# GpSimd clamps the weights' high words, and one fixed order of all operations: forgetting attention with two feed-forward layers

## The chip, the cores and the metric

The kernel runs on one core of a Trainium2 chip. The metric is the device time of one execution in microseconds (us). One further execution is recorded by the hardware profiler; its span runs from the first to the last instruction on the core, and all rows below come from it.

## The reference

```python
def _attn_ref(q, k, v, s):                      # batch 4, 8 heads, 576 positions, 64 wide
    scores = scale * np.matmul(q, k.transpose(0, 1, 3, 2))
    cum = np.cumsum(np.maximum(s, 0.0), axis=-1)
    bias = -(cum[:, :, :, None] - cum[:, :, None, :])
    scores = np.where(causal, -1000000000.0, scores + np.minimum(bias, 0.0))
    ...
    return np.matmul(softmax(scores), v)

def _moe_ref(x, w_in, w_out):                   # 2304 tokens, 512 -> 2048 -> 512
    h = x @ w_in
    g = np.where(h >= 1, h, np.where(h <= -1, 0.0, (h + 1) ** 2 / 4))
    return g @ w_out

def _moe2_ref(x, w_a, w_b, w_out):              # 512 -> 1536 -> 512
    return ((x @ w_a) * (x @ w_b)) @ w_out
```

The weights come as 64-bit floating point. The program has to turn each into a 32-bit value on the chip, and it multiplies in a reduced 32-bit format: a value is split into a high and a low part, and a product takes three passes (high by high, high by low, low by high).

## The kernel before, in words

The work is three stages that overlap: attention for four batches of 576 positions (ATT), layer one for batches 0 and 1, then 2 and 3, and layer two in the same pairs (PHASES). Attention goes by heads: a head's q and k are loaded in 64 rows each, scores come out of TensorE in row blocks of 116 (lines 982 and 991, the first head's at 961 and 971), VectorE adds the mask and takes the row's least value (line 1014), ScalarE takes the exponential (line 1029), TensorE turns the result (line 1055), ScalarE or VectorE copies it out, and TensorE multiplies it with v (line 1098). From batch 2 on the finished rows are parked in memory and fetched again. In the first heads q and k go to TensorE as they are; later ones are split into high and low parts, by a conversion on ScalarE or GpSimd (line 675 is GpSimd's) and a subtraction on VectorE (line 938).

The layers are tiled by blocks of 128 hidden columns and by batch. A plain product is in line 1351. For some phases a product of 2 by 2 blocks is done with seven products in place of eight (line 1508): it needs sums of the input blocks, "forms" (made at lines 1466 to 1479), and sums of the weight blocks, "sets" (lines 1429 to 1434), and its seven results are put together by ScalarE and VectorE (lines 1525 to 1540). y is summed in SBUF (line 1612).

**The weights.** values_of (from line 1261) makes 32-bit values of one weight tile of 128 by 512. SP loads the 64-bit words into one of two places of a tile `conv`. ScalarE scales the low words (line 1292) and takes the absolute value of the high words (line 1294). VectorE clamps that between two limits (line 1296, `wclamp`), shifts it (1298), puts the sign in (1300), and adds the low word's part (1302). load_unit then splits the value into high and low (a cast on ScalarE or GpSimd, and a subtraction on VectorE at line 1330) and stores it, so that later phases load it without a conversion (`whl`). keep_raw stores the value itself. There are 68 such tiles, from 13.8 to 681.0 us. For layer one GpSimd also makes sums (lines 1245 and 1252). The tile for the values has two places, and the one for the low words has one.

**The order of the work.** Nothing is issued as it is written: `op` records each operation with the engines that it may run on and their costs, what it reads and writes, and a key from the table KEYS. There are 4,604 operations, and 112 of them may run on either of two engines (mostly ScalarE or GpSimd for casts, and ScalarE or VectorE for copies). `Plan.run` keeps a clock for each engine, worked out from the costs. At each step it looks, for each engine, through up to 30 (LOOK) operations that are ready, in order of their keys, asks for places in their tiles (Room.find, Banks.find), and issues the one that can start first. The keys are thus preferences, and the plan's clocks decide; an operation for two engines goes to the one that can take it first. Each engine then runs its own instructions in the order of issue. SP starts all loads and stores, 618 of them, and waits at the head of its queue for the place or the value that a transfer needs.

Where the plan sees TensorE standing for more than 2 us (FILL_FROM), it puts in matmuls of zeros (`fill`, line 763). At the start there are 12 of the same kind (line 809). The plan adds up to 0.5 us to a VectorE operation marked `port` that begins while GpSimd is at work.

Of the kernel before, what the change touches and what calls it, by code (L numbers as in the profile page):

```python
# [44 lines left out]
LOOK = 30  # L45
# [4 lines left out]
    -46.11, -45.72, -39.66, -46.69, -57.55, -59.4, -56.04, -53.81, -44.56, -25.01, 13.24, 16.59, 24.15, 38.58, 45.28, 37.13, 42.56, 33.78, -57.18,  # L50
    -50.52, -31.43, -35.21, -34.65, -32.74, -24.3, -25.04, -29.4, -50.41, 4.82, 8.8, 14.61, 19.55, 6.46, 8.15, 20.64, 10.74, 3.69, 7.7, 15.87, 22.6,
    6.82, 9.05, 19.81, 21.57, 3.47, 9.85, 13.94, 21.33, -44.91, -5.67, -39.52, -3.58, -34.78, -3.2, -42.69, -6.95, -49, -0.1, -35.09, -3.13, -4.51,
    -4.13, 6.33, -5.33, 13.97, 21.29, 12.47, 12.1, 20.26, 15.12, 10.52, 15.27, 15.16, 19.71, 19.27, 15.23, 16.72, 20.55, 22.35, -15.22, 2.3, -14.99,
    3.83, 0.58, 12.31, 3.97, 8.12, 6.13, 3.35, 9.65, -1.29, 10.75, 10.41, -1.96, 6.13, 32.03, 16.69, 14.21, 39.19, 42.64, 33.41, 44.85, 22.96, 16.18,
    3.78, 33.95, 9.53, 17.76, 18.01, 18.93, 17.39, 15.29, 21.48, 18, 18.32, 24.48, 23.68, 18.74, 26.16, 31.41, 23.41, 31.3, 21.59, 15.71, 20.23, 20.2,
    21.89, 27.66, 27.38, 28.16, 26.5, 27.83, 30.34, 32.19, 7.5, 8.54, 12.39, 17.34, 24.92, 30.83, 30.7, 26.56, 33.78, 62.22, 24.92, 29.96, 30.15,
    29.06, 35.74, 38.18, 31.05, 33.72, 40.23, 28.23, 35.36, 25.88, 31.71, 31.12, 28.75, 32.54, 34.37, 32.14, 33.45, 33.79, 32.87, 34.73, 35.8, 28.08,
    39.72, 51.79, 36.92, 42.88, 40.47, 40.03, 63.22, 63.61, 50.35, 55.27, 45.07, 66.12, 4.68, 30.82, 34.42, 31.83, 33.79, 37.18, 37.81, 33.92, 42.45,
    34.2, 34.73, 41.93, 29.32, 32.17, 35.55, 35.88, 37.84, 53.62, 41.86, 34.58, 45.47, 52.47, 47.3, 49.65, 47.66, 53.67, 47.59, 56.45, 34.97, 31.09,
    31.02, 63.46, 40.36, 43.13, 43.1, 41.69, 40.02, 35.97, 41.77, 36.29, 44.98, 53.74, 38.2, 40.1, 39.37, 38.98, 49.82, 35.41, 28.27, 39.35, 30.19,  # L60
    48.82, 51.73, 45.29, 86.7, 48.99, 87.18, 50.86, 98.48, 52.54, 90.5, 57.23, 59.37, 36.65, 59.32, 66.24, 64.7, 66.85, 75.86, 69.08, 38.41, 39.3,
    42.42, 58.92, 19.71, 51.32, 57.22, 55.6, 41.45, 45.4, 67.54, 49.1, 49.91, 51.38, 50.01, 51.21, 55.65, 47.88, 49.6, 47.56, 54.2, 53.52, 57.64,
    50.6, 58.48, 58.4, 57.77, 59.16, 59.25, 62.82, 59.31, 45.63, 45.32, 37.43, 41.76, 57.93, 50.56, 56, 55.9, 48.96, 49.79, 56.09, 50.71, 59.97, 56.1,
    52.7, 65.04, 56.78, 55.07, 59.19, 58.36, 59.73, 60.56, 61.13, 61.1, 63.13, 64.23, 57.95, 59.15, 62.09, 63.15, 61.91, 56.32, 62.52, 61.54, 64.55,
    72.33, 40.14, 39.97, 66.28, 83.48, 72.91, 70.44, 51.46, 64.33, 62.3, 43.01, 66.78, 55.99, 54.16, 52.65, 59.4, 57.74, 53.82, 55.88, 61.76, 62.22,
    64.21, 62.58, 71.71, 67.62, 66.91, 58.78, 62.27, 61.43, 60.49, 63.07, 62.38, 68.54, 64.37, 71.1, 73.37, 69.15, 69.69, 70.85, 69.44, 48.71, 48.24,
    50.63, 64.2, 63.95, 64.56, 60.47, 67.79, 63.68, 66.66, 67.58, 74.58, 63.81, 73.31, 78.28, 68.8, 70.72, 70.88, 75.42, 61.14, 83.49, 68.94, 99.75,
    77.62, 87.21, 69.19, 86.41, 73.37, 86.79, 75.64, 91.76, 71.77, 83.29, 88.14, 84.7, 76.73, 93.72, 97.96, 100.6, 123.75, 124.45, 116.61, 114.63,
    105.58, 72.95, 73.48, 74.13, 74.29, 11.62, 17.68, 76.99, 86.6, 80.99, 76.28, 41.42, 84.47, 85.97, 84.62, 88.57, 90.99, 83.27, 98.68, 100.82,
    99.04, 99.89, 104.26, 101.37, 87.54, 79.89, 87.96, 79.4, 85.79, 94.98, 88.86, 102.14, 112.47, 103.93, 101.45, 92.09, 91.25, 92.23, 91.45, 74.84,  # L70
    64.62, 66.5, 67.37, 15.19, 22.88, 69.62, 75.56, 74.22, 96.12, 91.55, 96.81, 103.14, 76.8, 75.99, 83.43, 96.23, 99.89, 100.63, 99.4, 108.88,
    103.21, 97.26, 101.77, 104.73, 93.59, 71.05, 77.84, 67.27, 90.89, 97.58, 97.72, 93.55, 99.29, 102.74, 101.71, 97.81, 101.09, 105.61, 110.28,
    113.17, 111.59, 111.21, 123.39, 114.14, 123.27, 120.72, 118.67, 131.24, 134.85, 77.19, 73.91, 76.07, 78.5, 119.81, 99.61, 82.68, 94.07, 102.28,
    119.27, 69.6, 99.96, 100.92, 98.79, 99.63, 98.71, 114.33, 104.04, 102.52, 104.03, 104.57, 101.75, 100.84, 108.42, 106.57, 105.58, 103.1, 100.91,
    105.38, 101.71, 110.41, 106.85, 113.64, 108.8, 112.16, 108.86, 112.06, 106.96, 83.67, 85.51, 83.63, 85.47, 92.75, 94.29, 101.18, 102.36, 98.83,
    107.29, 107.32, 131.07, 111.75, 107.66, 105.68, 107.78, 116.1, 106.05, 118.75, 119.12, 119.04, 117.49, 115.45, 114.67, 129.55, 110.61, 107.04,
    113.05, 103.56, 114.89, 110.15, 106.36, 116.4, 105.22, 112.23, 107.83, 114.58, 106.64, 110.57, 104.2, 93.45, 115.23, 120.86, 125.08, 130.76,
    137.55, 135.92, 144.81, 165.18, 149.75, 102.16, 103.03, 113.69, 102.17, 102.9, 113.95, 112.51, 107.47, 102.27, 138.94, 101.43, 116.55, 126.98,
    120.59, 120.8, 130.48, 123.95, 123.07, 127.17, 136.29, 126.6, 135.51, 132.23, 128.5, 135.58, 131.72, 115.08, 106.74, 114.86, 113.18, 117.38,
    116.36, 113, 120.38, 122.04, 123.21, 123.17, 121.42, 108.12, 108.72, 109.94, 111.53, 119.99, 119.65, 127.95, 111.49, 135.2, 131.84, 130.3, 135.93,  # L80
    130.68, 126.36, 126.68, 134.88, 130.44, 128.59, 134.52, 132.29, 131.49, 147.24, 134.01, 138.83, 130.58, 148.14, 150.72, 134.08, 141.8, 151.68,
    144.98, 137.76, 144.37, 143.27, 149.78, 141.08, 149.12, 146.53, 150.86, 151.55, 153.79, 120.68, 133.07, 134.55, 134.03, 162.07, 161.05, 157.58,
    157.26, 159.28, 143.71, 131.34, 145.57, 145.64, 127.95, 127.44, 117.72, 144.13, 149.16, 161.69, 127.37, 149.51, 157.82, 165.83, 135.77, 138.2,
    166.31, 141.07, 140.22, 165.27, 147.53, 155.07, 175.32, 147.73, 148.66, 178.99, 151.57, 161.32, 156.92, 153.86, 152.62, 153.3, 158.61, 156.96,
    158.51, 162.77, 158.95, 169.03, 98.59, 81.85, 100.79, 103.95, 144.02, 142.7, 134.54, 154.81, 138.84, 147.06, 156.07, 146.8, 160.61, 158.7, 151.64,
    158.13, 157.88, 145.1, 165.1, 159.1, 149.29, 153.92, 163.9, 155, 160.61, 163.79, 168.82, 165.69, 158.39, 167.74, 184.37, 156.42, 167.52, 160.03,
# [1679 lines left out]
```

## Time and profile before

| | |
|---|---|
| median of 3 runs | 1028.62 us (1025.46 to 1031.27) |
| profiled execution, its time | 1028.6 us |
| profiled execution, its span | 1026.9 us |
| mean granted clock of TensorE | 0.998 |
| TensorE busy | 1012.2 us |
| VectorE busy | 815.9 us |
| ScalarE busy | 613.1 us |
| GpSimd busy | 95.2 us |

A row of the trace names a line of the kernel, an engine (PE is TensorE's multiplication, PEld its weight load, DVE VectorE, ACT ScalarE, POOL GpSimd, SP the queue of loads and stores), the tile written and the tile read, and the shape. "before" an arrow stands idle time and what ended it. Idle time costs only where the engine is the one that sets the end.

### The profile page before, as it was taken

The page shows a single profiled execution, that of the slowest core. Times are in us where ns is not written, and L with a number is a line of the kernel's source. Part 1 is how long each engine was busy: PE and PEld are TensorE (multiplying, and loading weights), DVE is VectorE, ACT ScalarE, POOL GpSimd, SP SyncE. Part 2 cuts the span into 40 slices and gives each one's busy share as a digit, 9 for nine tenths or more (in the row PEclk, how much of TensorE's full clock was granted, in tenths as well). Part 3 has the DMA queues.
Part 4 walks back from the last instruction along what each step waited for, and adds up shares of the span by engine and source line. Part 5 has one row for each costly group of instructions (what it writes and reads, how often), then busy time and mean ns, then how long its engine had stood idle before and what let it go on. Part 6 is the DMA issues. An engine that isn't in the chain of part 4 may idle for free.

```text
span 1026.9 us, 20033 instructions
## 1 busy us (share of the span) xinstructions
PE 1012.2 (99%) x7548; PEld 960.1 (94%) x7548; DVE 815.9 (79%) x1629; ACT 613.1 (60%) x1307; POOL 95.2 (9%) x130
## 2 busy tenths in 40 slices
PE   8999999999999999999999999999999999999998
PEld 5768889899999988999999999999999999999998
DVE  7888888767788979878888998897788985766563
ACT  5888888787686974786666535554333444452230
POOL 3232342010202202000000000000000000000000
PEclk9999999999999999999999999999999999999999
DMA  5676678876676668668373553443133331030012
GB/s 147 207 239 190 197 239 279 250 235 201 184 244 229 212 203 282 230 199 272 138 237 104 170 177 116 133 165 112 42 126 109 113 106 41 22 124 22 21 63 93
DMA packets 83321, 166.25 MB, mean 162 GB/s; under 512 B 9260, under 2 KB 40236, under 8 KB 83224
## 3 DMA queue, kind: packets, MB, share of 16 engines
q1 hardware_dynamic: 83128, 164.82, 49.0%
q8 instruction: 59, 0.97, 0.4%
q14 instruction: 38, 0.31, 0.1%
q10 hardware_dynamic: 96, 0.15, 0.0%
HBM read 119.57 MB, written 44.82 MB: 160 GB/s over the span
## 4 chain that ended last, share of the span: by engine, by line
PE 89%; DVE 3%; DMA 3%; ACT 2%; POOL 1%; issue 1%; SPq 1%; POOLq 0%; DVEq 0%
PE pp L1351 29%; PE pp L1508 20%; PE ps L1508 15%; PE ps L1351 11%; PE ps L1098 4%; PE ps L1055 4%; PE ps L991 2%; PE ps L982 2%; PE pp L991 1%; PE pp L982 1%; DMA conv<-in_w_in 1%; DMA qkraw<-in_qk 1%; DMA v<-in_v 1%; POOL g L1466 1%; SPq L683 1%
## 5 line engine op out<-in xcount | busy, mean ns | idle before, releaser
L1351 PE MATMUL pp<-g,whl 128*128 128x288 f32 x1788 | 261.1, 297 | 2.4 <-DVE y L1612 1.7
L1351 PEld LDWEIGHTS pp<-g,whl 128*128 128x128 f32 x1788 | 243.6, 188 | 3.6 <-issue 2.1
L1508 PE MATMUL pp<-form,set 128*128 128x288 f32 x1536 | 235.0, 297 | 0.1
L1508 PEld LDWEIGHTS pp<-form,set 128*128 128x128 f32 x1536 | 213.6, 188 | 1.3 <-DVE ct L1540 0.4
L1508 PE MATMUL ps<-form,set 128*128 128x288 f32 x1152 | 175.2, 296 | 0.8 <-DVE ct L1527 0.5
L1508 PEld LDWEIGHTS ps<-form,set 128*128 128x128 f32 x1152 | 160.3, 188 | 1.3 <-DVE ct L1527 0.8
L1351 PE MATMUL ps<-g,whl 128*128 128x288 f32 x900 | 137.5, 296 | 0.0
L1351 PEld LDWEIGHTS ps<-g,whl 128*128 128x128 f32 x900 | 125.4, 188 | 0.3
L1351 PE MATMUL pp<-x,whl 128*128 128x288 f32 x720 | 105.7, 300 | 0.3 <-DVE mx L1014 0.3
L1351 PEld LDWEIGHTS pp<-x,whl 128*128 128x128 f32 x720 | 98.3, 190 | 1.9 <-issue 0.6
L1029 ACT ACTIVATE p<-p,mx 116x232 f32<-116x232 f32 (+4 forms) x140 | 81.5, 583 | 8.9 <-DVE mx L1014 8.2
L1527 DVE TENSOR_TENSOR ct<-ps,ct 128x288 f32<-128x288 f32 x128 | 57.7, 455 | 35.8 <-ACT ct L1536 17.3
L1536 ACT COPY ct<-ps 128x576 f32<-128x576 f32 x64 | 41.1, 641 | 66.6 <-PE ps L1508 52.2
L1433 ACT CAST set<-sums 128x1024 fp32r<-128x1024 f32 (+1 forms) x56 | 53.6, 957 | 44.7 <-DVE sums L1429 22.2
L1549 ACT CAST g<-ct 128x576 fp32r<-128x576 f32 x80 | 51.2, 674 | 44.5 <-PE pp L1351 19.1
L671 ACT COPY pt<-ps 116x448 f32<-116x448 f32 (+5 forms) x175 | 64.5, 399 | 14.5 <-PE ps L1055 13.0
L1434 DVE TENSOR_TENSOR set<-sums,set 128x1024 fp32r<-128x1024 f32 (+1 forms) x56 | 61.9, 1106 | 8.9 <-ACT set L1433 8.1
L1612 DVE TENSOR_TENSOR y<-pp,y 128x576 f32<-128x576 f32 x70 | 52.7, 754 | 18.6 <-PE pp L1351 18.3
L1550 DVE TENSOR_TENSOR g<-ct,g 128x576 fp32r<-128x576 f32 x80 | 58.1, 754 | 8.4 <-ACT g L1549 7.7
L1540 DVE TENSOR_TENSOR ct<-pp,ct 128x576 f32<-128x576 f32 x64 | 48.2, 754 | 17.0 <-PE pp L1508 16.6
L1014 DVE CUSTOM_DVE_ANT_0 p<-ps,hide 116x348 f32<-116x348 f32 (+3 forms) x112 | 49.5, 453 | 15.1 <-PE ps L991 11.2
L1055 PE MATMUL ps<-ident,p 116*116 116x116 f32 (+2 forms) x420 | 60.1, 264 | 1.2 <-ACT xraw L1108 0.5
(123 smaller groups left out, 1390.7 us busy)
## 6 DMA issues: line engine op xcount, KB each, us to landing
whl<-keep_out SPq DMA_DIRECT2D x48, 512.0 KB
qkraw<-in_qk SPq DMA_DIRECT2D x108, 144.0 KB
conv<-in_w_out SPq DMA_DIRECT2D x28, 512.0 KB
keep_out<-whl SPq DMA_DIRECT2D x28, 512.0 KB
conv<-in_w_in SPq DMA_DIRECT2D x16, 512.0 KB
keep_in<-whl SPq DMA_DIRECT2D x16, 512.0 KB
g<-park SPq DMA_DIRECT2D x22, 288.0 KB
conv<-in_w_a SPq DMA_DIRECT2D x24, 256.0 KB
```

Of the source, the lines that this page charges most:

```text
L671: nc.scalar.copy(o, i)
L1014: nc.vector.tensor_tensor_reduce(out=psl(pref.t)[:r].rearrange("q (g n) -> q g n", g=parts), in0=pv()[:r, :parts, :w], in1=hide[:r, lag : ...
L1029: nc.scalar.activation(p, p, AF.Exp, bias=mx.t[:r], scale=-1.0, accum_out=sm.t[:r, h % 2, i : i + 1])
L1055: nc.tensor.transpose(pt.t[: rows[j], (j - j0) * QT : (j - j0) * QT + r], psl(pref.t)[:r, QT * j : QT * j + rows[j]], ident[:r, :r],)
L1351: nc.tensor.matmul(bank_of(ps, a)[:, :HN], w(wu), x(xu)[:, a * HN : (a + 1) * HN], start=(k == 0 and t == 0), stop=(k == len(terms) - 1 an ...
L1433: op({ACT: act(256 * n)}, k, lambda e: nc.scalar.copy(part(0, j0, n), src()), reads, slots, name="sethi")
L1434: op({DVE: tt(256 * n)}, k, lambda e: nc.vector.tensor_tensor(part(1, j0, n), src(), f32(part(0, j0, n)), op=ALU.subtract), reads, slots, ...
L1508: nc.tensor.matmul(at(to), by_pair(st.t)[:, w, wu, g], forms[b, layer, g].t[:, x, xu], start=fresh and k == 0, stop=k == len(terms) - 1, s ...
L1527: op({DVE: tt(HN)}, k, lambda e: nc.vector.tensor_tensor(cut(f, f), at(to), cut(f, f), op=ALU.add), [to, *shared], [(c, q)], name="partadd")
L1549: op({ACT: act(S)}, k, lambda e, f=f: nc.scalar.copy(g[f].t[:, 0], t.t[:, f]), need[f], [(g[f], 0)], name="ghi")
L1550: op({DVE: tt(S)}, k, lambda e, f=f: nc.vector.tensor_tensor(g[f].t[:, 1], t.t[:, f], f32(g[f].t[:, 0]), op=ALU.subtract), [*need[f], (g[f ...
L1612: nc.vector.tensor_tensor(o, i, o, op=ALU.add)
```

## The change

Two things change. The clamp of the high words (line 1296) is issued on GpSimd and not on VectorE, with the same two limits and the same shape, and it is no longer marked `port`. And the plan no longer searches: KEYS holds a whole number for each operation, every number once, TURNS says for each of the 112 operations with two engines which it takes, and `Plan.run` issues all operations in the order of their numbers. It still keeps the clocks, which now serve to choose places in tiles and banks and to find gaps for the matmuls of zeros; an operation that would come ahead of one that it needs, or for which there is no place, stops the build.

The numbers are new, not those of the former plan's outcome. Set side by side, TensorE's 1,318 operations are 5 places from their former place on average and 35 at most. GpSimd's operations go from 121 to 188, VectorE's from 1,412 to 1,344, ScalarE's from 1,135 to 1,136; of the two-engine operations 49 change sides, 22 of them copies between ScalarE and VectorE.

```diff
-LOOK = 30
...
 KEYS = (
...
+TURNS = (
+    "0100011001011011000101000100100101000001001010011001111101111011011111011111110011011001101110011011000111111101"
 )
...
         key = KEYS[len(self.ops)]
         o.engs, o.key, o.fn, o.move, o.name, o.port, o.lat = engs, key, fn, move, name, port, lat
+        o.by = 0
+        if len(engs) > 1:
+            o.by = int(TURNS[self.turn])
+            self.turn += 1
...
-        while True:
-            best = None
-            for e, todo in ready.items():
...
-            (t, key, o, places), e = best
+        for count, o in enumerate(sorted(self.ops, key=lambda o: o.key)):
+            assert o.waits == 0, f"{o.name} ({count}) comes too early"
+            e = list(o.engs)[o.by]
+            t = max(clock[e], o.ready)
+            places = []
+            ahead = {}
+            for r in o.refs:
+                if r.t is None:
+                    r.room.now = clock[e]
+                    at = r.room.find(r, ahead.get(id(r.room), 0))
+                    assert at is not None, f"{o.name} ({count}) has no place"
+                    ahead[id(r.room)] = ahead.get(id(r.room), 0) + 1
+                    places.append((r, at[1]))
+                    t = max(t, at[0])
             for r, at in places:
                 r.room.take(r, at)
...
-        op({DVE: ts(512)}, k, lambda e: vec.tensor_scalar(wr.t, wr.t, HIGH_MOST, HIGH_LEAST, op0=ALU.min, op1=ALU.max),
-            (), [(wr, 0)], name="wclamp", port=True)
+        op({POOL: pool(512)}, k, lambda e: nc.gpsimd.tensor_scalar(wr.t, wr.t, HIGH_MOST, HIGH_LEAST, op0=ALU.min, op1=ALU.max),
+            (), [(wr, 0)], name="wclamp")
```

## Rows read from the trace of the kernel before

**Rows 1.** The page's table of engines: busy time, share of the span, instructions.

```profile
PE 1012.2 (99%) x7548; PEld 960.1 (94%) x7548; DVE 815.9 (79%) x1629; ACT 613.1 (60%) x1307; POOL 95.2 (9%) x130
```

**Rows 2.** Busy time of each engine by stretch; columns as its first line says.

```profile
core 0: us, PE busy (x) PEld busy (x) DVE busy (x) ACT busy (x) POOL busy (x), PEclk, DMA share, GB/s
0.00:425.00 425.00, 413.64 (x3054) 362.69 (x3055) 353.36 (x797) 328.47 (x801) 95.23 (x130) 1.00 0.69 223
425.00:1000.00 575.00, 575.00 (x4320) 574.17 (x4319) 453.62 (x819) 283.34 (x506) 0.00 (x0) 1.00 0.36 120
76.00:79.40 3.40, 3.15 (x15) 2.65 (x16) 3.05 (x11) 1.69 (x6) 0.04 (x1) 0.50 0.81 236
389.00:407.00 18.00, 16.30 (x114) 14.23 (x112) 17.93 (x36) 7.75 (x16) 2.22 (x2) 1.00 0.75 252
```

**Rows 3.** TensorE's waits: for whom, us in total, times, longest.

```profile
PE ps L1098 <- DMA v<-in_v: 1.7, 1, 1.7
PE pp L1351 <- DVE y L1612: 1.7, 1, 1.7
PE ps L809 <- DVE zeros L804: 1.3, 1, 1.3
...
PE ps L991 <- DVE early L1387: 0.9, 1, 0.9
PE pp L1351 <- DVE mx L1014: 0.9, 2, 0.7
PE ps L961 <- DMA qkraw<-in_qk: 0.8, 1, 0.8
PE ps L1508 <- DVE ct L1527: 0.5, 1, 0.5
...
PE ps L1351 <- DVE mx L1014: 0.2, 1, 0.2
```

**Rows 4.** TensorE's timeline: start, us, instructions merged, idle time before them.

```profile
1.26 4.27 PE L809 MATMUL ps<-zeros 128*128 128x512 bf16 x12 [1.26 <-DVE zeros L804]
...
76.25 1.43 PE L1098 MATMUL ps<-pt,v 116*64 116x232 f32 x8 [1.74 <-DMA v<-in_v]
...
389.79 3.63 PE L763 MATMUL ps<-zeros 128*128 128x512 bf16 x16
...
401.47 3.42 PE L1351 MATMUL pp<-g,whl 128*128 128x288 f32 x24 [1.70 <-DVE y L1612]
...
1020.18 3.34 PE L1351 MATMUL ps<-g,whl 128*128 128x288 f32 x24
```

**Rows 5.** The clamp, line 1296: ns least/median/most, first and last start.

```profile
L1296 DVE TENSOR_SCALAR conv<-conv x68: 366/421/954, 13.8 to 681.0; 128x512 f32<-128x512 f32 x68
```

**Rows 6.** Busy time of line 1296 alone by stretch.

```profile
0.00:425.00 425.00, 20.13 (x44) 1.00 0.69 223
425.00:700.00 275.00, 10.12 (x24) 1.00 0.53 174
375.00:425.00 50.00, 1.65 (x4) 1.00 0.74 257
```

**Rows 7.** GpSimd's copies and conversions of 128x512: ns least/median/most.

```profile
L1245 POOL COPY g<-conv x8: 610/612/616, 41.1 to 338.4; 128x512 f32<-128x512 f32 x8
...
L675 POOL CAST whl<-conv x10: 609/614/1877, 22.2 to 167.0; 128x512 fp32r<-128x512 f32 x10
```

**Rows 8.** The chain that ended last, 104 to 109 us: start, us, what.

```profile
104.97 0.08 issue
105.06 1.75 POOL qk L675
106.81 0.02 issue
106.83 1.35 DVE qk L938
```

**Rows 9.** Waits of SP's queue and of GpSimd: us in total, times, longest.

```profile
SPq L683 <- DVE conv L1300: 119.5, 39, 12.6
...
POOL qk L675 <- PE pp L991: 34.7, 4, 19.0
```

**Rows 10.** VectorE, lines 1330, 1298 and 1612: ns least/median/most.

```profile
L1330 DVE TENSOR_TENSOR whl<-conv,whl x44: 668/686/1228, 25.3 to 690.9; 128x512 fp32r<-128x512 f32 x44
...
L1298 DVE TENSOR_SCALAR conv<-conv x68: 403/423/1296, 15.0 to 681.7; 128x512 uint32<-128x512 uint32 x68
...
L1612 DVE TENSOR_TENSOR y<-pp,y x70: 697/757/769, 176.1 to 1020.4; 128x576 f32<-128x576 f32 x70
```

**Rows 11.** The chain that ended last, around 70 us: start, us, what.

```profile
69.28 6.83 DMA v<-in_v
76.11 0.14 issue
76.25 1.43 PE ps L1098 x8
```

More of the change, by code (lines that the diff above doesn't have):

```diff
@@ L423 @@
 class Op:
-    __slots__ = ("engs", "key", "fn", "refs", "after", "waits", "ready", "move", "done", "name", "n", "port", "lat")
+    __slots__ = ("engs", "key", "fn", "refs", "after", "waits", "ready", "move", "name", "n", "port", "lat", "by")
 class Plan:
@@ L433, in __init__ @@
         self.ops = []
+        self.turn = 0
         self.writer = {}
@@ L449, in op @@
         o.engs, o.key, o.fn, o.move, o.name, o.port, o.lat = engs, key, fn, move, name, port, lat
-        o.after, o.ready, o.done, o.n = [], 0.0, False, len(self.ops)
+        o.after, o.ready, o.n = [], 0.0, len(self.ops)
+        o.by = 0
+        if len(engs) > 1:
+            o.by = int(TURNS[self.turn])
+            self.turn += 1
         before = set()
@@ L481, in run @@
             r.sort()
-        clock = {}
-        ready = {}
+        clock = dict.fromkeys(self.LAT, 0.0)
         moved = shared = cold = 0.0
-        count = 0
-        def push(o):
-            for n, (e, c) in enumerate(o.engs.items()):
-                clock.setdefault(e, 0.0)
-                bisect.insort(ready.setdefault(e, []), (o.key + 2.0 * n, o.n, o))
-        for o in self.ops:
-            if o.waits == 0:
-                push(o)
-        while True:
-            best = None
-            for e, todo in ready.items():
-                found = None
-                looked = 0
-                for key, _, o in todo:
-                    if looked >= LOOK:
-                        break
-                    t = max(clock[e], o.ready)
-                    places = []
-                    ahead = {}
-                    for r in o.refs:
-                        if r.t is None:
-                            r.room.now = clock[e]
-                            at = r.room.find(r, ahead.get(id(r.room), 0))
-                            if at is None:
-                                places = None
-                                break
-                            ahead[id(r.room)] = ahead.get(id(r.room), 0) + 1
-                            places.append((r, at[1]))
-                            t = max(t, at[0])
-                    if places is None:
-                        continue
-                    looked += 1
-                    if found is None or t < found[0] - 0.02:
-                        found = (t, key, o, places)
-                    if t <= clock[e] + 0.05:
-                        break
-                if found and (best is None or found[:2] < best[0][:2]):
-                    best = (found, e)
-            if best is None:
-                break
-            (t, key, o, places), e = best
@@ L528, in run @@
             for r, at in places:
                 r.room.take(r, at)
-            for n, e2 in enumerate(o.engs):
-                todo = ready[e2]
-                todo.pop(bisect.bisect_left(todo, (o.key + 2.0 * n, o.n)))
             end = t + o.engs[e]
@@ L551, in run @@
             o.fn(e)
-            o.done = True
-            count += 1
             for r in o.refs:
@@ L559, in run @@
                 a.ready = max(a.ready, end + self.LAT[e] + (SLACK if "SP" in a.engs else 0.0))
-                if a.waits == 0:
-                    push(a)
-        stuck = [(o.name, o.key, o.waits) for o in self.ops if not o.done]
-        assert not stuck, f"{len(stuck)} operations have no place: {sorted(stuck, key=lambda x: x[1])[:8]}"
 def act(n):
```

1 line of the change is left out of this document (added), and 435 rows, old and new, of the table KEYS.

## The prediction

> **What bounds the kernel now.** I began with the page's table of engines: TensorE is busy for 1012.2 us of a span of 1026.9 [rows 1]. So I then asked where the other 14.7 us are, by busy time per stage [rows 2]. From 425 to 1000 us the row shows 575.00 of 575 us: TensorE never stands there, and neither a lighter VectorE nor another order can shorten that stretch; a new order can only open a gap in it. Before 425 us it is 413.64 of 425, so 11.4 us are lost there, while VectorE is busy for 353 of those 425 us (83%). That is the stage with attention in it, and the change can only pay there.
>
> Then the list of TensorE's waits with the timeline around the longest [rows 3, 4]. Three things don't count as reachable: 1.26 us ahead of the first matmul, 0.80 us on the first load of q and k, and the tail after the last matmul (1020.18 + 3.34 = 1023.52 us, so 3.4 us, with an addition and the last store in it) [rows 3, 4]. That leaves 14.7 - 1.26 - 0.80 - 3.4 = 9.2 us of idle time inside. Two losses are hidden in busy time. Sixteen matmuls of zeros at 389.8 us (line 763) take 3.63 us; the plan puts them where it foresees a long gap of TensorE [rows 4]. And in 76.0 to 79.4 us, right behind the 1.74 us wait for a load of v, the granted clock is 0.50, the lower of the two levels, 1.2 GHz; half of 3.4 us is 1.7 us lost [rows 2, 4]. Together 9.2 + 3.6 + 1.7 = 14.5 us: that is about all that another order of the same work could gain. 0.5% of the time, about what a measurement of this kernel can tell from no change, is 5.1 us, a good third of that.
>
> **The clamp, part by part.** Removed from VectorE: 68 clamps, median 421 ns, in all 30.25 us, 20.13 of them before 425 us and 10.12 from 425 to 700 [rows 5, 6]. The last 24 are worth nothing in time, as TensorE is full there. The 44 early ones are 5% of the stage.
>
> Added to GpSimd: 68 clamps of 128x512. No row shows a two-step tensor_scalar of that kind on GpSimd. The nearest row is a plain copy of the same size on that engine, 610 to 616 ns; a conversion of the same size takes 609 to 1877 [rows 7]. From below, the VectorE clamp's 366 ns bounds it [rows 5]; from above 1877. I take 0.65 us, next to the copy, since a clamp also has one input and one output: 68 x 0.65 = 44 us, 44 x 0.65 = 29 us of it before 425 us. GpSimd is busy for 95 us there, and then for 124 of 425 [rows 2]; later it is empty. With the upper bound it would be 95 + 83 = 178 of 425, still no bound. I cost this work itself at nothing: it lies beside TensorE. If the cover goes, it is 0.65 - 0.42 = 0.23 us for each weight tile.
>
> Two more crossings per tile, ScalarE to GpSimd and GpSimd to VectorE. The chain around 105 us shows such crossings: some 0.1 us before the GpSimd conversion starts and 0.02 after it [rows 8]. A tile's chain so grows by 0.23 + 0.12 = 0.35 us, at most 1.5 + 0.1 = 1.6 us. What waits for a tile's chain is the next weight load on SP, which stands behind it 39 times, 119.5 us in all [rows 9]; that cover is large as long as the clamp is not itself kept waiting (the slower rival below).
>
> What VectorE gets back is less than 30 us. The 128x512 subtraction at line 1330 has median 686 ns but a maximum of 1228, and the shift at line 1298 goes from 423 to 1296, whereas the addition that reads PSUM at line 1612 stays within 697 to 769 [rows 10]. In the early stage, where GpSimd works, some VectorE instructions on SBUF are thus stretched by about 0.54 us. The rows don't say how often; I take it that one clamp in three does that: 44 / 3 x 0.54 = 8 us come back, so VectorE's net relief before 425 us is 20 - 8 = 12 us.
> The Trainium skill (GPSIMD Engine Reference, Key points) says that GpSimd shares its SBUF interfaces with VectorE and contends with instructions in a two-port mode or with two SBUF inputs. The rows above agree in kind; by that rule every clamp that finds such an instruction would stretch it, and the relief would be gone (44 x 0.54 = 24 us against 20).
>
> How much of the relief reaches TensorE? Of its waits, those that VectorE ended are 1.7 + 0.9 + 0.9 + 0.5 us and one of 0.2: 4.2 us, without the first [rows 3]. VectorE is busy for 17.93 of the 18 us around the change to layer one's seven-product form, 389 to 407 us, where the largest of them lies [rows 2, 4]; but only 4 clamps stand in all of 375 to 425 [rows 6]. I give the clamp alone 1.5 us.
>
> **The order.** What a step issues stays the same but for the clamps and the zeros: the same 4,604 operations, the same loads and stores. What changes is their order on every queue, SP's 618 loads and stores included, and which engine takes 49 of the 112 that may run on two. Counting places in the two orders, TensorE's 1,318 operations stand 5 places from where they stood on average, at most 35, in the late, full stage as much as in the early one. Attention ends at the same place; the first seven-product step stands two places earlier, and the subtractions for the second half of its forms some eight places earlier. On GpSimd the queue grows from 121 to 188 operations.
> The trace of before can't show a new order, so I bound it: on one side all 14.5 us come back; on the other none does, and waits of the dearest kind seen (1.74 us and the low clock's 1.7 behind it, 3.4 us) open anew, three of them 10 us. My value goes by the kinds of loss. The wait for v with the low clock, 3.4 us, is a load issued late behind others, at 69.28 us, that landed after 6.83 us [rows 11]; a few places on SP's queue settle it, and I count 2.5 of it back. Of the gap that the plan itself foresees, zeros 3.6 and the wait of 1.7 behind them, 5.3 us, I count 2.5 back: VectorE is full there, so no more. Of the rest, 14.5 - 3.4 - 5.3 = 5.8 us in small waits, 2 us. Against that I put 1 us of new waits somewhere. Order: 2.5 + 2.5 + 2 - 1 = 6.0 us.
>
> **The sum.** 1.5 + 6.0 = 7.5 us. The profiled execution took 1028.6 us (span 1026.9 and 1.7 around it), as much as the median of the runs, 1028.62. So 1028.6 - 7.5 = 1021.1 us, 0.7% faster.
>
> **Rivals.**
> 1. The stalls move rather than go: the new order takes back the 2.5 us at the wait for v but closes no gap at 389 us, where VectorE is full, and opens as many small ones as it closes; GpSimd's contention eats the relief. For it: VectorE's 17.93 of 18 us, and that the places move in the full stage too, where there is only loss to be had. Against it: the losses sit in few places, and the plan knows the largest, as the zeros show. Time: 1028.6 - 2.5 = 1026.1 us, the same by the bound above.
> 2. Slower: the clamp queues behind a GpSimd instruction that itself waits. GpSimd stood four times for TensorE with a conversion of k and q at its head, 34.7 us, the longest 19.0 [rows 9]. A clamp behind such a head makes its tile late; the next weight load waits at SP for that tile [rows 9], and behind it on SP stand the loads of q, k and v. Each such event then costs what the late load of v cost, 1.74 + 1.7 = 3.4 us. The gain of 7.5 us outweighs two events; with three, and the gain halved because the late tiles also spoil the order, it is 1028.6 - 3.7 + 10.2 = 1035.1 us. It decides when the head waits longer than the slack of a load, several microseconds. Against it: from 150 us on GpSimd has few conversions, and an order that is written down can put the clamp ahead of them.
> 3. The clamp's relief is the main thing: VectorE was the bound in the whole early stage, and its waits go altogether (4.2 us), together with the low clock, the zeros and half the rest: 1028.6 - 4.2 - 3.4 - 3.6 = 1017.4. Faster, at the lower end.
> That the change doesn't do what it says is hardly open: the edit names the engine.
>
> **How the numbers follow.** The forecast 0.42, rival 3 0.14, rival 1 0.27, rival 2 0.17. Rival 1 and the forecast overlap at the bound of 1023.5 us, and I move nothing for it: faster 0.56, same 0.27, slower 0.17. The range reaches down to 1014 us, which is all that can be had, and up to 1033, which holds rival 1 with one event of 3.4 us and more; it leaves most of rival 2 out. The forecast's own range, by which the order returns 3 to 10 us, is 1017 to 1024.
>
> **What would show it.** Right: 68 clamps of about 0.65 us at GpSimd; VectorE some 22 us less busy; fewer than 16 matmuls of zeros; no stretch with a clock of 0.5 at 76 us; TensorE before 425 us standing for 5 us or less in place of 11.4, and 575 of 575 busy later. Rival 1: the same sum of waits under other names. Rival 2: GpSimd's clamp waiting behind a conversion, SP standing for the weight tiles much longer than 119.5 us, a new stretch at the low clock. The forecast is wrong if the late stage shows gaps, or if a clamp takes over 1 us and VectorE is no less busy.

## The result and the profile after

The changed kernel takes 1035.22 us (median of 6 runs, 1034.92 to 1035.46), the kernel before 1027.69 beside it (1025.46 to 1031.27). The ratio is 1.008, 95% interval 1.0057 to 1.0102: 0.8% slower, where 0.7% faster was forecast, and outside the range of 1014 to 1033. The profiled execution took 1035.46 us, its span 1033.7.

The page's table of engines of the kernel after, against [rows 1]:

```profile
PE 1018.8 (99%) x7559; PEld 959.3 (93%) x7561; DVE 798.0 (77%) x1572; ACT 611.2 (59%) x1309; POOL 147.2 (14%) x197
```

Everything that the edit says is there. VectorE is 17.9 us less busy and GpSimd 52 us more. TensorE seems busier by 6.6 us: 11 more matmuls of zeros are in that number, and parts of waits (below). Its idle time is nearly the same, 14.9 us and 14.7, so the loss can't be read from it.

Busy time by stretch, kernel after, against [rows 2]; the stretch from 80 to 183 us is added:

```profile
core 0: us, PE busy (x) PEld busy (x) DVE busy (x) ACT busy (x) POOL busy (x), PEclk, DMA share, GB/s
0.00:425.00 425.00, 416.11 (x3056) 360.17 (x3059) 341.42 (x751) 326.70 (x798) 129.68 (x173) 1.00 0.68 220
425.00:1000.00 575.00, 572.93 (x4285) 569.87 (x4285) 443.01 (x798) 282.47 (x508) 17.50 (x25) 1.00 0.36 122
80.00:183.00 103.00, 96.98 (x736) 82.66 (x736) 87.97 (x185) 83.57 (x217) 45.97 (x57) 1.00 0.68 216
76.00:79.40 3.40, 3.40 (x29) 3.40 (x28) 2.66 (x4) 2.51 (x6) 0.61 (x1) 1.00 0.61 167
```

The same stretch from 80 to 183 us in the kernel before:

```profile
80.00:183.00 103.00, 100.67 (x788) 90.22 (x787) 89.01 (x198) 85.78 (x222) 35.80 (x44) 1.00 0.68 219
```

Three things are to be seen. The late stage, 575.00 of 575 before, now has 2.07 us of idle time. From 80 to 183 us TensorE works 96.98 us of 103 and not 100.67. And at 76 us, where the old kernel waited for v and then ran at half clock, TensorE is busy throughout at the full clock.

TensorE's waits in the kernel after, against [rows 3]:

```profile
PE pp L1409 <- DVE ct L1428: 1.4, 2, 1.0
PE ps L664 <- ACT pt L572: 1.3, 1, 1.3
PE ps L710 <- DVE zeros L705: 1.3, 1, 1.3
PE ps L1252 <- DVE row L1053: 1.2, 1, 1.2
PE pp L1409 <- DVE y L1513: 1.1, 1, 1.1
PE ps L892 <- DVE qk L839: 1.0, 2, 0.8
PE ps L956 <- ACT p L930: 0.9, 2, 0.7
```

The single waits for v and for a y of line 1351 [rows 3] are gone. In their place stand as many small ones, most of them on VectorE. Their places are in TensorE's timeline, against [rows 4]; the row at 408.55 us answers to the old wait at 401 us:

```profile
97.73 1.02 PE L664 MATMUL ps<-zeros 128*128 128x512 bf16 x3 [1.35 <-ACT pt L572]
...
132.85 0.31 PE L956 MATMUL ps<-ident,p 116*116 116x116 f32 x1 [0.74 <-ACT p L930]
...
177.06 1.21 PE L1252 MATMUL ps<-x,whl 128*128 128x288 f32 x7 [1.22 <-DVE row L1053]
...
391.76 5.34 PE L664 MATMUL ps<-zeros 128*128 128x512 bf16 x24
...
408.55 1.04 PE L1409 MATMUL pp<-form,set 128*128 128x288 f32 x6 [1.11 <-DVE y L1513]
...
937.77 1.07 PE L1409 MATMUL pp<-form,set 128*128 128x288 f32 x6 [1.01 <-DVE ct L1428]
```

Zeros: 27 where 16 were, 24 of them in one row of 5.34 us at 391.8 us. The change of form at 390 to 408 us costs more than before, not less.

**Where the time went.** Total busy time can't show this, so I laid the two TensorE timelines over each other at equal work: the matmuls in order without the zeros, each with its duration, and then the difference of the two times when the same amount is done (weighing a matmul by its undisturbed spacing in place of its duration moves the figures below by up to 0.7 us and changes no sign). After minus before: -4.2 us at 77 us (the wait for v and its low clock, and 0.7 from the first 25 us); -0.4 at 103; +3.9 at 183; +1.8 at 425; +6.4 at the end. So the change gained 4.2 us, lost 8.1 between 80 and 183 us (some 3 of them between 95 and 103 us, where the row at 97.73 us stands), gained 2.1 up to 425, and lost 4.6 in the full stage. Most of that lies in five steps, at 499 us (0.4), 511 (0.7), 654 (0.4), 939 (1.7) and 1006 (0.4). That is more than the 2.07 us of idle time there: 24 matmuls in a row take 3.34 us [rows 4] and 12 take 1.75, so one follows the other every 0.13 us, while the record of one is 0.29 us long. The first 0.16 us of each wait thus hide under the record of the matmul before; the wait of 1.01 us at 937.77 us makes its matmul 1.17 us late.

The clamp, its neighbours on VectorE, and the addition that reads PSUM in the kernel after (least/median/most), against [rows 5, 10]:

```profile
L1197 POOL TENSOR_SCALAR conv<-conv x68: 607/616/3484, 12.5 to 683.2; 128x512 f32<-128x512 f32 x68
...
L1199 DVE TENSOR_SCALAR conv<-conv x68: 364/422/1369, 14.7 to 688.3; 128x512 uint32<-128x512 uint32 x68
...
L1201 DVE SCALAR_TENSOR_TENSOR conv<-conv x68: 677/692/1152, 15.2 to 692.7; 128x512 uint32<-128x512 uint32 x68
...
L1513 DVE TENSOR_TENSOR y<-pp,y x59: 740/751/759, 189.3 to 1026.7; 128x576 f32<-128x576 f32 x59
```

The clamp's median is 616 ns, its mean 759 (51.5 us in all). Instructions of VectorE that work on SBUF are stretched while GpSimd works, line 1199 up to 1369 ns: GpSimd was at work beside each of the 12 of its 68 that took over 15% more than the median, and without GpSimd beside it none took more than 429 ns. Line 1513, which reads PSUM, is not stretched.

Waits for and around the clamp, kernel after, against [rows 9]:

```profile
POOL conv L1197 <- ACT conv L1195: 363.3, 53, 51.3
...
DVE conv L1199 <- POOL conv L1197: 9.5, 12, 2.0
...
SPq L584 <- DVE conv L1201: 80.2, 40, 6.4
```

GpSimd stands ready for the clamp most of the time (363 us of waiting for ScalarE's step ahead of it), VectorE waits for a clamp 9.5 us in all and 2.0 us at most, and SP waits less for the weight tiles than before, 80.2 us against 119.5. The clamp is not what is late.

### The profile page after: what moved, and what is told of

Same layout as the page of the kernel before. It is cut to its first block, busy times and chain, and to the rows that moved or that the text cites. A ratio compares the mean times of both kernels' runs of the same rounds, so it can differ in the third digit from the quotient of the medians.

```text
span 1033.7 us, 20083 instructions
## 1 busy us (share of the span) xinstructions
PE 1018.8 (99%) x7559; PEld 959.3 (93%) x7561; DVE 798.0 (77%) x1572; ACT 611.2 (59%) x1309; POOL 147.2 (14%) x197
## 4 chain that ended last, share of the span: by engine, by line
PE 89%; DVE 5%; ACT 2%; issue 1%; DMA 1%; POOL 1%; SPq 0%; DVEq 0%; POOLq 0%; ACTq 0%
PE pp L1252 27%; PE pp L1409 19%; PE ps L1252 14%; PE ps L1409 14%; PE ps L956 4%; PE ps L999 4%; PE ps L892 2%; PE ps L883 2%; PE pp L892 1%; PE pp L883 1%; DVE qk L839 1%; DVE ct L1428 1%; DVE p L915 1%; DVE whl L1231 1%; PE ps L664 1%
## 5 line engine op out<-in xcount | busy, mean ns | idle before, releaser
L1252 PE MATMUL pp<-g,whl 128*128 128x288 f32 x1596 | 235.7, 296 | 0.5 <-DVE ct L1441 0.3
L1252 PEld LDWEIGHTS pp<-g,whl 128*128 128x128 f32 x1596 | 218.4, 188 | 2.0 <-DVE ct L1441 1.2
L1409 PE MATMUL ps<-form,set 128*128 128x288 f32 x1152 | 177.3, 295 | 0.0
L1252 PE MATMUL ps<-g,whl 128*128 128x288 f32 x1092 | 165.6, 295 | 0.0
L1252 PEld LDWEIGHTS ps<-g,whl 128*128 128x128 f32 x1092 | 151.6, 188 | 0.6 <-ACT ct L1437 0.2
L1197 POOL TENSOR_SCALAR conv<-conv 128x512 f32<-128x512 f32 x68 | 51.5, 759 | 412.7 <-ACT conv L1195 363.3
L572 ACT COPY pt<-ps 116x232 f32<-116x232 f32 (+5 forms) x175 | 65.8, 399 | 22.7 <-PE ps L956 21.1
```

Source lines behind the costliest of these rows:

```text
L572: nc.scalar.copy(o, i)
L1197: op({POOL: pool(512)}, k, lambda e: nc.gpsimd.tensor_scalar(wr.t, wr.t, HIGH_MOST, HIGH_LEAST, op0=ALU.min, op1=ALU.max), (), [(wr, 0)], ...
L1252: nc.tensor.matmul(bank_of(ps, a)[:, :HN], w(wu), x(xu)[:, a * HN : (a + 1) * HN], start=(k == 0 and t == 0), stop=(k == len(terms) - 1 an ...
L1409: nc.tensor.matmul(at(to), by_pair(st.t)[:, w, wu, g], forms[b, layer, g].t[:, x, xu], start=fresh and k == 0, stop=k == len(terms) - 1, s ...
```

## Experiments

Two theories: what costs is the clamp on GpSimd, by its length or by contention; or it is the new order, and then the question is where.

**The clamp in two orders.** First the new table with the clamp on VectorE:

```diff
-        op({POOL: pool(512)}, k, lambda e: nc.gpsimd.tensor_scalar(wr.t, wr.t, HIGH_MOST, HIGH_LEAST, op0=ALU.min, op1=ALU.max),
+        op({POOL: pool(512)}, k, lambda e: nc.vector.tensor_scalar(wr.t, wr.t, HIGH_MOST, HIGH_LEAST, op0=ALU.min, op1=ALU.max),
```

> The new order with its places and the plan's clocks unchanged, and only the clamp issued on VectorE at the same point of the table. Theory G (the clamp on GpSimd costs the time: VectorE instructions on SBUF are stretched beside it and wait for it): 1021 to 1027 us, faster than the changed kernel by 8 or more, and VectorE's shift at line 1199 back at 0.42 us. Theory O (the new order is the worse one by itself): 1033 to 1036 us, as the changed kernel.

Measured: 1041.39 us, ratio 1.0124 (1.0093 to 1.0154), slower than either theory allowed. Then the old order, as the old plan finds it, with the clamp issued on GpSimd:

```diff
-        op({DVE: ts(512)}, k, lambda e: vec.tensor_scalar(wr.t, wr.t, HIGH_MOST, HIGH_LEAST, op0=ALU.min, op1=ALU.max),
+        op({DVE: ts(512)}, k, lambda e: nc.gpsimd.tensor_scalar(wr.t, wr.t, HIGH_MOST, HIGH_LEAST, op0=ALU.min, op1=ALU.max),
```

> The kernel before with its own order, and only the clamp issued on GpSimd at the same point. Theory G: 1033 to 1040 us, the whole loss without the new order. Theory O: 1026 to 1030 us, as before.

Measured: 1031.3 us (1025.38 to 1035.98), between the two expected ranges, but ratio 1.0012 (0.9976 to 1.0047) beside its own runs of the kernel before: no difference that shows. Third, the new table with a clamp of one column on GpSimd, which leaves 511 of 512 columns unclamped (so does one further run below):

```diff
+... nc.gpsimd.tensor_scalar(wr.t[:, :1], wr.t[:, :1], HIGH_MOST, HIGH_LEAST, op0=ALU.min, op1=ALU.max),
```

> The changed kernel with a GpSimd clamp of one column in place of 512 (511 columns stay unclamped): the crossing between the engines stays, the 0.62 us of work and of shared access go. Theory G by contention: 1022 to 1029 us. Theory G by the crossing and its waits: still over 1032. Theory O: 1033 to 1036.

Measured: 1033.01 us, ratio 1.0032 (1.0009 to 1.0055). That fits the order, and the crossing between the engines as well, which is still in this run; but without the crossing to GpSimd (the first run) the new order is slower still, and in the old order the crossing costs nothing that shows (the second). Fourth, the clamp twice, one after the other:

```diff
+... lambda e: [nc.gpsimd.tensor_scalar(wr.t, wr.t, HIGH_MOST, HIGH_LEAST, op0=ALU.min, op1=ALU.max) for _ in range(2)],
```

> The changed kernel with each clamp issued twice in a row on GpSimd, so that its work and its contention double. Theory G: 1040 us or more, about as much on top as e3 takes off. Theory O: at most 1037 us.

Measured: 1046.56 us, ratio 1.0173 (1.0136 to 1.021), over 1040 as the theory of the clamp had it, but it adds five times what the one-column clamp took off. GpSimd's groups by line in that run (x count, busy us, mean ns, idle before):

```profile
L1197 POOL TENSOR_SCALAR conv<-conv 128x512 f32<-128x512 f32 x136 | 99.9, 736 | 388.9 <-ACT conv L1195 349.5 <-DVE y L1514 16.1 <-DVE ct L1429 14.1
```

What follows: in the old order the engine of the clamp makes no difference. In the new one, GpSimd's clamp is 6 us better than VectorE's, and all its cost but the crossing, length and contention together, is 1035.2 - 1033.0 = 2.2 us (2.5 by the two spans). A second clamp costs 11 us more, so a tight order takes one of these but not two. With nearly no clamp at all the new order is still slower than the old kernel. The clamp on GpSimd is thus a smaller part of the loss; the rest is the order's.

**New and old order joined.** Four tables take the new order for a part of the 4,604 operations and the old plan's for the rest, all with the clamp on GpSimd (where the old order stands, the plan still prices it as VectorE's, so that the order keeps). Where the two orders meet is called the joint.

```diff
 KEYS = (
...
-        op({POOL: pool(512)}, k, lambda e: nc.gpsimd.tensor_scalar(wr.t, wr.t, HIGH_MOST, HIGH_LEAST, op0=ALU.min, op1=ALU.max),
-            (), [(wr, 0)], name="wclamp")
+        op({POOL: pool(512), DVE: ts(512)}, k, lambda e: nc.gpsimd.tensor_scalar(wr.t, wr.t, HIGH_MOST, HIGH_LEAST, op0=ALU.min, op1=ALU.max),
+            (), [(wr, 0)], name="wclamp", port=True)
```

The first 500 operations new (to 80 us):

> Clamp on GpSimd; the first 500 operations of the new order (to about 80 us), then all others in the old order. Theory O1 (the new order loses in the attention stage between 80 and 205 us, and again late): 1025 to 1028 us with the clock at 1.0. Rival O2 (the start of the new order is what costs, and its lateness is carried on): 1031 or more.

Measured: 1027.03 us, ratio 0.9978 (0.9954 to 1.0002). The first 1,240 new (to 205 us):

> Clamp on GpSimd; the first 1240 operations of the new order (to about 205 us), then the old order. O1: 1031 to 1036 us, 5 to 8 more than with the first 500. Rival O3 (the loss is made late, where TensorE is full and any gap is lost): 1025 to 1029.

Measured: 1036.73 us, ratio 1.0082 (1.0047 to 1.0118). The first 2,600 new (to 480 us):

> Clamp on GpSimd; the first 2600 operations of the new order (to about 480 us), then the old order. O1: 1029 to 1033 us (2 to 3 us come back between 205 and 425 us as in the trace of the changed kernel, and the 4 us lost late are avoided). O3: 1025 to 1029.

Measured: 1037.62 us, ratio 1.0092 (1.006 to 1.0124). The first 2,575 old, the rest new:

> Clamp on GpSimd; the first 2575 operations of the old order (to about 470 us), then the new order. O1: 1028 to 1031 us in runs with the clock at 1.0, that is 3 to 5 more than the old order alone. O3: 1033 to 1036.

Measured: 1036.73 us (1031.75 to 1042.05), ratio 1.0074 (1.0046 to 1.0102). The last three can't be read by their times alone, since a joint has a price of its own. TensorE's timeline with the joint at 480 us:

```profile
497.47 4.85 PE L664 MATMUL ps<-zeros 128*128 128x512 bf16 x11 [3.01 <-DVE y L1513]
```

At equal work that joint costs 8.4 us, and the one at 205 some 5.5. In the run with the old order first, the profile has another loss far ahead of the joint, a stretch at the lower clock near its start (the profile of the old order with GpSimd's clamp throughout has the same, 0.50 there):

```profile
24.00:28.00 4.00, 4.00 (x16) 2.04 (x15) 1.66 (x7) 1.76 (x6) 1.14 (x3) 0.50 0.03 5
```

So the times of these three can't decide between the expectations. What they still show, at equal work and apart from the joints: with the new order up to 205 us, the stretch from 80 to 205 loses 5.2 us, and with the new order up to 480 the end of that stage stands 1.7 us behind, both as in the kernel after. And the run with the old order first shows the late loss without the early part of the new order: behind its joint, from 520 us on, it loses 3.4 us against the kernel before, in the same steps as the kernel after (3.2 there), with the same wait at the largest of them:

```profile
941.10 1.06 PE L1409 MATMUL pp<-form,set 128*128 128x288 f32 x6 [1.01 <-DVE ct L1428]
```

Nor does it hang on the clamp, as the late stage of the run with the one-column clamp has gaps too, while the kernel before and the run with the old order from 80 us on are busy there for 575.00 of 575 us:

```profile
425.00:1000.00 575.00, 573.15 (x4289) 570.32 (x4288) 440.50 (x797) 282.13 (x508) 6.29 (x24) 1.00 0.37 122
```

The first of the four is the cleanest measurement of the new order's parts: it takes the new order's good start and then the old order with GpSimd's clamp. Its late stage and its stretch from 80 us, and a wait that neither kernel has at that place:

```profile
425.00:1000.00 575.00, 575.00 (x4320) 574.14 (x4319) 448.37 (x795) 283.02 (x505) 19.54 (x24) 1.00 0.36 120
80.00:183.00 103.00, 99.47 (x771) 88.00 (x770) 88.21 (x193) 87.08 (x224) 43.07 (x55) 1.00 0.73 231
...
92.23 0.69 PE L956 MATMUL ps<-ident,p 112*116 112x112 f32 x5 [1.29 <-ACT p L930]
```

Against it, at equal work, the kernel after loses 6.0 us between 80 and 183 us, gains 3.7 from 300 to 425 and loses 4.4 after. The run with the one-column clamp loses 3.7 in the first of these, the one with the clamp on VectorE 6.5. So in 80 to 183 us some 2.3 us are the clamp's, and 3.7 are what the new order loses there beyond this run. But this run loses too: against the kernel before it is 3.9 us ahead at 77 us, 1.3 at 127 and 0.3 at 467, and most of the first step lies between 80 and 93 us, where it waits for ScalarE at 92.23 us. Whether the joint is to blame or a TensorE that comes early there was not tried. Against the kernel before, the order's part of the 8.1 us is thus 5.8 and not 3.7.

**Two more forms of the good start**, the clamp on VectorE behind the joint, and a clamp of one column throughout:

```diff
-        ... lambda e: nc.gpsimd.tensor_scalar(wr.t, wr.t, HIGH_MOST, HIGH_LEAST, op0=ALU.min, op1=ALU.max),
+        ... lambda e: eng[e].tensor_scalar(wr.t, wr.t, HIGH_MOST, HIGH_LEAST, op0=ALU.min, op1=ALU.max),
```

> The new order for the first 500 operations, 8 clamps on GpSimd among them, then the old order with the clamp on VectorE. If the good parts of both add up (no late load of v and no low clock at 76 us, the old order behind it): 1024 to 1026.5 us, below both kernels. If the clamp on GpSimd was a gain in the old order, more than the 1027.0 of the same order with all clamps on GpSimd.

Measured: 1027.3 us, ratio 0.9973 (0.9948 to 0.9998).

> The same order as e5, with a clamp of one column (511 stay unclamped), so that VectorE is relieved of 30 us and next to nothing is added on GpSimd. If relief of VectorE pays in an order that was found with the clamp on VectorE: 1022 to 1025 us. If it does not, because waits there end elsewhere: 1025.5 to 1028, as e5.

Measured: 1026.28 us, ratio 0.9958 (0.9934 to 0.9983). With the old order from 80 us on, a clamp on VectorE, on GpSimd, or hardly any gives 1027.3, 1027.0 and 1026.3 us. Taking the 60 clamps off VectorE that the first of these two leaves there, 26.7 us, is worth about 1 us, and the ranges of the runs overlap. The run with VectorE's clamp lies 0.27% below the kernel before: little, and its interval ends just below 1. Nor is it the faster kernel at full clock: its four runs with a mean granted clock of 1.0 took 1027.3 to 1027.8 us, and the 24 such runs of the kernel before (of 86 beside these experiments) a median of 1025.9. What it gains is that it has no slower ones: 1028.4 us at most, against 1039.4.

**Without zeros.** The kernel after with

```diff
-FILL_FROM = 2.0
+FILL_FROM = 1e9
```

> The changed kernel without the 27 matmuls of zeros in the plan's gaps. Theory Z (they fill time in which TensorE has nothing to do, except the three at 97.7 us, which hold back a product with v by 1 us): 1033.5 to 1035.5 us. Rival C (TensorE's clock falls to the lower level behind the empty gap at 392 us): 1036 or more, with a stretch at 0.5.

Measured: 1036.77 us, ratio 1.0066 (1.004 to 1.0092), 1.5 us above the kernel after. The profiled execution is the fastest of its 12 and took 1035.39 us, as long as the kernel after; ten of the others have a mean granted clock of 0.994 to 0.996 against its 0.998, so what they lose more is not in this trace. TensorE's timeline where the 24 zeros were, and the clock just behind (PEclk is the third number from the end):

```profile
393.73 0.40 PE L1252 MATMUL ps<-g,whl 128*128 128x288 f32 x1 [1.63 <-ACT g L572]
396.59 1.88 PE L1252 MATMUL ps<-g,whl 128*128 128x288 f32 x8 [2.47 <-DVE g L1298]
398.26 4.35 PE L1252 MATMUL pp<-g,whl 128*128 128x288 f32 x24
```

```profile
396.60:400.00 3.40, 3.40 (x16) 3.40 (x17) 3.40 (x9) 0.81 (x2) 2.55 (x1) 0.57 0.69 281
```

The zeros cover a gap that is there anyway, 1.63 and 2.47 us in a row. Without them the granted clock falls behind it to a mean of 0.57 for 3.4 us, and the 24 matmuls of 398.26 us take 4.35 us and not 3.35. In this execution that is made up again by 409 us, as the wait for y of the kernel after (1.11 us at 408.55) is not there; at the end the two are equal. The 24 zeros are a sign of the loss and not its cause.

**Places in the queues.** VectorE runs its instructions in the order of issue. In the kernel after, VectorE's timeline around 130 and 936 us:

```profile
128.52 1.70 DVE L1298 TENSOR_TENSOR g<-third,g 128x576 fp32r<-128x576 f32 x1
130.25 1.71 DVE L839 TENSOR_TENSOR qk<-qkraw,qk 64x1152 fp32r<-64x1152 f32 x1
131.99 0.28 DVE L915 CUSTOM_DVE_ANT_0 p<-ps,hide 116x116 f32<-116x116 f32 x1
...
935.39 1.22 DVE L1335 TENSOR_TENSOR set<-sums,set 128x1024 fp32r<-128x1024 f32 x1 [1.65 <-ACT set L1334]
936.54 0.81 DVE L1428 TENSOR_TENSOR ct<-ps,ct 128x288 f32<-128x288 f32 x2
```

and what GpSimd does at 130 us:

```profile
127.99 2.76 POOL L576 CAST qk<-qkraw 128x1152 fp32r<-128x1152 f32 x2
130.83 1.60 POOL L1197 TENSOR_SCALAR conv<-conv 128x512 f32<-128x512 f32 x1
```

A row minimum of 0.28 us (line 915) stands behind two subtractions (lines 1298 and 839) of 1.7 us each, which take 0.75 and 1.36 undisturbed, beside GpSimd's cast and clamp. The exponential waits for the minimum, and TensorE for the exponential (the row at 132.85 us of its timeline above, 0.74 us). At 936 us the part of the row minimum is played by an addition (line 1428) behind a subtraction for a set (line 1335) that itself waits 1.65 us for ScalarE; TensorE waits 1.01 us for the addition.

That gave a testable claim. Three operations or pairs of the kernel after were moved a few places: the row copy (line 1053) ahead of a subtraction for q and k at 176 us, the cast and subtraction for g ahead of five forms at 395 us, and this set behind two additions.

```diff
 KEYS = (
...
```

> The changed kernel with three operations or pairs moved up to 16 places: the conversion and subtraction of g that TensorE waits for at 397 us ahead of five subtractions for the forms, a weight set's subtraction at 935 us behind two additions that free a bank, a copy of ten rows at 177 us ahead of a 1.36 us subtraction. Theory Q (TensorE is held up by what VectorE is given first, and the places in the queue are what costs): 1030.5 to 1033 us, the stalls at 175, 392 and 937 us shorter by 1.2, 2 and 0.8 us. Rival F (VectorE's queue is simply full there, so that another instruction comes late instead): 1034.5 to 1036.

Measured: 1034.08 us, ratio 1.0039 (1.0014 to 1.0064), 1.1 us below the kernel after and between the two expected ranges. At equal work it is 0.6 us ahead of the kernel after at 175 us and gains another 0.7 at 936 us, as the claim has it, though at 176 us it is half of what was expected. At 392 us it is ahead by 2.6 us and has given back 2.2 of that by 405 us; its TensorE timeline there:

```profile
401.54 1.04 PE L1252 MATMUL pp<-g,whl 128*128 128x288 f32 x6 [1.85 <-DVE y L1513]
...
407.12 1.05 PE L1409 MATMUL pp<-form,set 128*128 128x288 f32 x6 [1.37 <-DVE y L1513]
```

VectorE is busy for 32.7 of the 35 us from 390 to 425 there; what one instruction gains another loses. Then nine more moves of the same kind, between 90 and 165 us, on ScalarE and VectorE:

```diff
 KEYS = (
...
```

> The kernel of the run with three moves, and nine more operations moved between 90 and 165 us, each a few places: in each case a short instruction whose result TensorE waited for stood on ScalarE or VectorE behind one that nobody waited for (ScalarE: a copy of turned probabilities ahead of a relu and an exponential; VectorE: the reciprocals behind the subtraction for q and k, the subtractions for q and k, for x, for g and for a weight tile and one sign step behind the row minima that follow them). TensorE stood or ran zeros in these places for 1.35 + 1.02 at 97 us, 0.77 at 109, 0.74 at 132.9, 0.18 at 153, 0.39 at 157.9 and 0.21 at 164 us in the trace after the change, together 4.7 us. Theory Q (places in the in-order queues lose the time): most of it comes back, TensorE is 3 to 5 us further at 180 us than with three moves, and the time is 1029.5 to 1031.5 us against 1034. Rival F (the engines are full there, so what one instruction gains another loses): the waits turn up again under other names within 20 us, TensorE is less than 1.5 us further at 180 us and the time is 1033 to 1035. Rival L (what is gained at 180 us is lost again at the change of form near 390 to 410 us, where VectorE is full): further by 3 or more at 180 us, by less than 1.5 at 420, time 1032.5 to 1034.

Measured: 1037.15 us, ratio 1.0082 (1.0049 to 1.0115). None of the three expectations: at equal work it is 4.4 us *behind* the run with three moves at 180 us, and stays there to the end. Its profile is the slowest of its runs and that with three moves the fastest; by the medians nine moves cost 3.1 us. At equal work it loses 1.1 us around 100 us and 3.1 around 162 us. TensorE's timeline at both:

```profile
97.11 0.90 PE L999 MATMUL ps<-pt,v 116*64 116x232 f32 x8 [0.73 <-DMA v<-in_v]
99.61 1.93 PE L956 MATMUL ps<-ident,p 112*116 112x112 f32 x9 [1.60 <-DVE mx L915]
...
162.46 1.02 PE L664 MATMUL ps<-zeros 128*128 128x512 bf16 x4 [1.42 <-DVE mx L915]
...
168.29 0.68 PE L892 MATMUL ps<-qk 128*116 128x464 f32 x2 [0.71 <-ACT xraw L1009]
```

Behind the first of these the clock falls too, and the nine matmuls of 99.61 us take 1.93 us, where they took 1.42 with three moves only (PEclk third from the end):

```profile
99.00:102.40 3.40, 2.79 (x13) 2.64 (x14) 2.17 (x6) 2.56 (x8) 1.41 (x3) 0.57 0.50 137
```

VectorE's timeline ahead of the second:

```profile
158.82 0.52 DVE L915 CUSTOM_DVE_ANT_0 p<-ps,hide 116x348 f32<-116x348 f32 x1 [0.90 <-PE ps L892]
...
159.27 1.08 DVE L1298 TENSOR_TENSOR g<-early,g 128x576 fp32r<-128x576 f32 x1
160.27 1.21 DVE L1066 TENSOR_TENSOR x<-xraw,x 128x576 fp32r<-128x576 f32 x1
161.41 0.68 DVE L1201 SCALAR_TENSOR_TENSOR conv<-conv 128x512 uint32<-128x512 uint32 x1
162.01 0.38 DVE L915 CUSTOM_DVE_ANT_0 p<-ps,hide 116x232 f32<-116x232 f32 x1
```

At 97 us the copy that was moved ahead is no longer late, and TensorE waits for a load of v instead; behind that it waits 1.60 us more, where it did not wait at all with three moves only. At 158.82 us the row minimum, moved ahead, waits 0.90 us at the head of VectorE's queue for scores that TensorE has not made yet. Two subtractions and a sign step, which had run in that time, now take 2.7 us behind it, and the minimum after them comes at 162.01, for which TensorE waits 1.42 us and runs four zeros. So a few places decide: nine moves made 3 to 4 us. But a wait in the trace told which instruction was late, not where it could go: whatever it passes becomes late itself.

## Why the prediction was wrong

- **The bound.** That TensorE is the bound everywhere and full after 425 us was right, and so was the sentence that a new order can only open gaps there. I then let that count for at most 1 us "of new waits somewhere" in the sum. It was 4.6 us in that stage alone, and gaps in the late stage were the prediction's own sign of being wrong.
- **The clamp on GpSimd**, 0.65 us each: the median is 616 ns, the mean 759, as some are stretched up to 3484 ns. That the work itself costs nothing in the old order is shown (1031.3 and 1027.0 us); in the new order it is worth 2.2 us.
- **VectorE's relief.** 22 us less busy were to be seen, 17.9 came. In the old order with GpSimd's clamp, where nothing else changes sides, VectorE's busy time up to 1000 us falls by 17.7 us; of 30.25 us removed, 12.6 come back as stretched instructions, and I had 8. The Trainium skill (GPSIMD Engine Reference, Key points) has that contention, with two-port modes and two SBUF inputs; the runs agree in kind, a single instruction losing up to 0.95 us (line 1199, 1369 against 422 ns), and not with the relief being gone altogether, which I had worked out from it.
- **How much reaches TensorE**, 1.5 us: about 1 us, by the one-column clamp behind the good start; in the new order the clamp on GpSimd took 2.2 us instead. Cover that already hides a wait hides its relief too.
- **The wait for v**, 2.5 us: at its place it gave all of its 3.4 us. It is not kept in place: with the old order behind it and the clamp on VectorE, 4.2 us of lead at 77 us are 1.8 at 127, with a wait of 1.59 us for ScalarE at 92.20 us on the way, and 3.4 at the end in that execution, the fastest of its 12. I also took this loss for one that every run has. A stretch like that at 76 us takes 0.0017 off the mean granted clock (1.7 of 1027 us), so the 24 of 86 runs of the kernel before with a clock of 1.0 can't have had it; their median is 1025.9 us, and there at least the low clock's 1.7 us were not to be had.
- **The gap at 389 us**: 2.5 us were to come back, 16 zeros to become fewer. They became 27. The reason I gave for counting only half, that VectorE is full there, was the reason for all of it: moved work was given back within 15 us in the run with three moves.
- **The order**, +6.0 us: this is the step that failed. With hardly any clamp the new order is itself slower than the kernel before, 1033.0 us: by 5.3 us against its 1027.7, or by 0.32% beside its own runs. At equal work the new order's good start gives 4.2 us, and the rest loses more than that. I had bounded it by -10 us and +14.5 us and chosen a value by the *largest losses of the old trace*, that is by what there was to gain. What there was to lose I did not price: 80 to 183 us, where the old kernel stands for only 2.3 of 103 us with VectorE and ScalarE over 80% busy, and where nine small moves cost 3 to 4 us, and the full stage. Those two cost 8.1 + 4.6 = 12.7 us.
- **Rivals.** Rival 2 named 1035.1 us, the time that came, but by another mechanism: VectorE waits for a clamp 2.0 us at most, SP's wait for the weight tiles fell to 80.2 us, and the same clamps cost nothing in the old order. Rival 1 had the mechanism, stalls that move rather than go, "as many small ones as it closes", and the full stage "where there is only loss to be had"; its time, 1026.1, was 9 us too low, since it opened more than it closed. Rival 3 fell.

That the order loses, in the late stage without the clamp and without its early part, is shown. What stays open: of the 5.8 us that the order itself loses between 80 and 183 us, which places lose how much. One place (0.6 us at 176 us) is shown; the nine others were moved together, and lost. Of the late stage's 4.6 us, 0.7 are shown at the set of 936 us.

## What to carry to other kernels

An order that leaves the bounding engine idle for 1% of its time is itself a tuned object: a newly found one starts with the risk of all its places, and the stage to price is the full one, where it can only lose. Lay two traces over each other at equal work of the bounding engine before explaining a difference; a sum of waits hides that gains of 4 us and losses of 8 lie in different stages, and that a gain far from the end need not arrive there. Relief of an engine that only ends a wait now and then is to be taken at the size of those waits and not of the work removed: 26.7 us gave 1.

## What was not expected

- Both sides are lengthened where GpSimd and VectorE work side by side: GpSimd's clamp has a median of 616 and a maximum of 3484 ns, VectorE's line 1199 loses up to 0.95 us. VectorE was at work beside each of the 18 clamps that took over 640 ns, and the 9 without it took at most 622 ns.
- Right behind idle times of 1.63 and 2.47 us the granted clock was 0.57 on average over 3.4 us, so mostly at the lower of TensorE's two levels, 1.2 GHz; with matmuls of zeros in their place it stayed at 1.00. That alone did not make the profiled execution longer.
- The kernel before is itself uneven: with a mean granted clock of 1.0 its runs lie between 1024.3 and 1028.6 us, and with one of 0.99 around 1035, while the six runs of the changed kernel lie within 0.6 us.
- Nine moves of a few places each, on two engines that are not the bound, moved the end to the worse, by 3.1 us in the medians and 4.3 between the two profiles.
